# Transposing the first two batches of q and k head pair by head pair, in 64 by 64 blocks

## The chip, the core and the metric

The kernel runs on one core of a Trainium2 chip. The time is device time in microseconds (us) of one execution. Before the change the median of seven executions is 274.74 us (273.61 to 276.77). One further execution was recorded with the hardware profiler; it took 275.78 us, and its span, from the first to the last instruction, is 274.0 us. The clock granted to TensorE was 0.998 of full speed.

Engines are named as in the profile: PE (TensorE) does the matmuls, with PEld for its weight loads; DVE (VectorE), ACT (ScalarE) and POOL (GpSimd) do the rest of the arithmetic; SP (SyncE) issues nearly all of the transfers.

## What is computed

A causal attention over blocks of 64 positions is followed by a channel mix with two weight matrices and a gate. All inputs and the output are float32. The batch is 8, there are 8 heads, the sequence has 576 positions and a head has 64 columns.

```python
scores = (1 / sqrt(64)) * q @ k.T          # masked to block_i >= block_j
attn   = softmax(scores)
x      = (attn @ v)                        # heads side by side: 8 x 576 x 512
x_prev = x shifted by one position, zero first
xk = mu_k * x + (1 - mu_k) * x_prev
xr = mu_r * x + (1 - mu_r) * x_prev
kk = relu(xk @ w_k)                        # 512 -> 1024
out = sigmoid(xr @ w_r) * ((kk * kk) @ w_v)
```

## The kernel before

**Stages.** Scores are computed as keys by queries, so q and k are needed with the head's 64 columns on the partitions: the tile `t_qkt` holds, for each of four head pairs, 128 partitions, of which the upper 64 belong to one head and the lower 64 to another, for q and for k. The score matmuls (L774) contract over 64 partitions and alternate between the two heads of a pair, that is between the two halves of the partitions, writing two different PSUM banks. The exponential (L796, ACT) makes `t_e`, POOL sets masked pieces of it to zero (L805), and L839 multiplies it with v (`VO`; a column of ones gives the row sums). DVE normalises into `t_x` (L858, L859), TensorE transposes `t_x` (L913), and copies bring it to `t_xt`, which is cut into nine chunks of 512 positions. For each chunk `t_d` is the difference to the previous position (L952), `t_xk` and `t_xr` are two mixes of it (L964, DVE), and the three matrix products follow: L1000 with WK (then relu on ACT, L1010, and the square on DVE, L1016), L1029 with WR (tanh on ACT, L1039) and L1059 with WV, from which L1069 makes the output tile.

**Where q and k come from.** In batches 2 to 7 ("short rows") a transfer turns the rows: SP loads pieces, an engine casts them to bf16 (`NB`), and a transposing DMA writes `t_qkt`. In batches 0 and 1 (`LONGS = 2`, "long rows") TensorE does it. `add_long` loads with one transfer of 288 KB two neighbouring heads of q or k: partition `64*y + p` holds nine consecutive rows (576 numbers) of head y of the two. Two such transfers (x = 0 and 1) are cast into one tile `t_nl` of 128 x 9 x 128, x choosing the left or the right 64 of each 128 columns, so each cast writes pieces of 64 numbers. `add_long_qkt` then takes for each y the 64 partitions of that half and transposes nine blocks of 64 x 128 against a 64 x 64 identity (L704). Each result has 128 rows: 64 of the head of the first transfer, 64 of the head of the second. A pair in `t_qkt` therefore consists of heads from two transfers, and the function `heads` holds this other order of heads for these batches. An evacuation of 128 x 576 (L519 or L525) puts the nine blocks back into the order of positions.

**Order.** The kernel is a list of tasks, each with an engine, a planned duration, a rank, the tasks that it depends on and the ring buffers that it takes. `Plan.order` walks through planned time and gives each engine the free task of lowest rank; the result is a fixed order of instructions for each engine, and at run time every engine works its list strictly in order, waiting for data where it must. All ranks stand in the table `RANK`: `'loads'` is the order of SP's transfers for the first two batches and the weights (an entry such as `g0q` is two transfers, `v0` one of v, `wk3` a block of 256 KB of WK), the other entries move steps against each other, and `'eng'` chooses the engine for each cast, evacuation, copy and difference. L1000 of a chunk needs all four `t_xk` and four blocks of WK (for its first half, `wk0` to `wk3`), L1029 all four blocks of WR.

**Filler.** `fill` (L1098) is a pair of matmuls on the identity whose result nobody reads. 150 such tasks have the worst rank of all, so the plan puts them wherever TensorE has nothing else, until they are used up. They are 300 matmuls in TensorE's fixed list.

**Rings that matter here.** `ld` has ten buffers for all the float32 loads of q, k and weights, `vl` five for v; a transfer waits in SP's queue until its buffer is free, and the ones behind it wait too.

Of the kernel before, what the change touches and what calls it, by code (L numbers as in the profile page):

```python
# [9 lines left out]
FP = mybir.dt.float32  # L10
# [10 lines left out]
LONGS = 2  # L21
# [4 lines left out]
 'loads': ['g0q', 'v0', 'g0k', 'g1q', 'g1k', 'b1g1k', 'v4', 'wv3', 'wr3',  # L26
           'b1g0q', 'wk3', 'v2', 'v1', 'v3', 'b1g0k', 'wk2', 'wk4', 'wv5',
           'mu', 'b1v1', 'wk6', 'b1g1q', 'wr2', 'wv2', 'wk5', 'wv7',
           'b1v0', 'wv1', 'wr0', 'b1v2', 'b1v4', 'wk0', 'wk1', 'wv0',
           'wr1', 'b1v3', 'wk7', 'wv4', 'wv6'],  # L30
 'cast k': -51.0,
 'cast r': -434.5,
 'cast v': 313.0,
 'qkt0': [737.5, -314.0],
 'score0': [-705.0, -565.5, -372.0, -1059.0, -634.5, -690.5, -602.5,
            -488.0, -388.5, -812.5, -442.0, -834.5, -913.5],
 'av0': [-638.0, -695.5, -377.5, -465.0, -791.5, -541.5, -210.0, -635.5],
 'xt0': [-552.0, -461.5, -587.0, -627.5, -574.5],
 'mix0': [-254.0, 23.5, 351.5, 381.5],
 'pk0': [-136.5, 67.0, -206.0, -382.5, -79.5, -35.5, 48.0, -58.0],  # L40
 'pr0': [179.5, 182.0, -314.0, -81.5],
 'pv0': [15.0, -394.0, 22.5, 38.0],
 'qk': [38.0, 39.5, 41.5, 42.0],
 'v': 46.0,
 'qkt': [539.5, -136.5],
 'turn': 40.5,
 'av': -286.0,
 'xt': 6.0,
 'mix': 492.0,
 'xr': 423.5,  # L50
 'moe': 68.5,
 'eng': {'v32': 'DVE',
         'wk7': 'DVE',
         'qk201': 'POOL',
         'long0010': 'POOL',
         'v71': 'ACT',
         'd61': 'DVE',
# [3 lines left out]
         'd02': 'POOL',  # L61
         'd41': 'POOL',
         'v64': 'ACT',
         'qk511': 'POOL',
         'v72': 'POOL',
         'long0000': 'DVE',
         'd33': 'POOL',
         'qk611': 'POOL',
         'qk300': 'POOL',
         'd51': 'POOL',  # L70
         'v23': 'POOL',
         'long0110': 'DVE',
         'qk501': 'POOL',
         'd10': 'POOL',
         'ev0010': 'ACT',
         'v03': 'DVE',
         'd01': 'DVE',
         'long1110': 'POOL',
         'qk700': 'POOL',
         'v20': 'POOL',  # L80
         'v01': 'DVE',
         'qk601': 'POOL',
         'qk321': 'ACT',
         'v14': 'POOL',
         'qk620': 'ACT',
         'v51': 'DVE',
         'd20': 'POOL',
         'v41': 'POOL',
         'qk331': 'DVE',
         'qk430': 'POOL',  # L90
         'd32': 'POOL',
         'qk520': 'POOL',
         'long0001': 'ACT',
         'd53': 'DVE',
         'd81': 'POOL',
         'v73': 'POOL',
         'v40': 'POOL',
         'd31': 'DVE',
         'qk221': 'ACT',
         'd43': 'POOL',  # L100
# [3 lines left out]
         'qk730': 'ACT',  # L104
         'v21': 'POOL',
         'v54': 'POOL',
         'qk720': 'POOL',
         'wk6': 'DVE',
         'qk320': 'POOL',
         'd72': 'POOL',  # L110
         'v62': 'ACT',
         'd62': 'POOL',
         'qk500': 'POOL',
         'qk401': 'DVE',
         'v31': 'ACT',
         'd52': 'POOL',
         'long1111': 'POOL',
         'v63': 'POOL',
         'wk0': 'ACT',
         'qk411': 'POOL',  # L120
         'qk510': 'ACT',
         'long0011': 'ACT',
# [5 lines left out]
         'd82': 'DVE',  # L128
         'ev0000': 'ACT',
         'qk630': 'POOL',  # L130
         'v53': 'ACT',
         'v60': 'ACT',
         'v10': 'ACT',
# [3 lines left out]
         'qk421': 'POOL',  # L137
         'd11': 'POOL',
         'long1000': 'ACT',
         'qk310': 'POOL',  # L140
         'qk710': 'DVE',
         'long0111': 'ACT',
         'ev0101': 'ACT',
         'qk311': 'DVE',
         'wk2': 'DVE',
         'd71': 'POOL',
         'v52': 'POOL',
         'qk530': 'DVE',
         'qk220': 'DVE',
         'v04': 'POOL',  # L150
         'd73': 'POOL',
         'qk610': 'DVE',
         'd80': 'POOL',
         'long1100': 'ACT',
         'd60': 'POOL',
         'qk631': 'ACT',
         'qk600': 'DVE',
         'd83': 'POOL',
         'qk400': 'POOL',
         'v74': 'DVE',  # L160
         'v44': 'POOL',
         'v42': 'ACT',
         'long0100': 'DVE',
         'qk531': 'ACT',
         'long0101': 'DVE',
# [3 lines left out]
         'qk330': 'ACT',  # L169
         'd63': 'POOL',  # L170
         'qk231': 'POOL',
         'qk230': 'ACT',
         'v30': 'ACT',
         'd30': 'POOL',
         'qk711': 'POOL',
         'ev0001': 'ACT',
         'd50': 'POOL',
         'qk521': 'DVE',
         'long1101': 'POOL',
         'wk3': 'DVE',  # L180
         'qk431': 'POOL',
         'd00': 'POOL',
         'qk621': 'DVE',
         'qk731': 'POOL',
         'd03': 'POOL',
         'wk5': 'ACT',
         'qk410': 'DVE',
         'v02': 'POOL',
         'ev0011': 'ACT',
         'v34': 'ACT',  # L190
         'qk200': 'POOL',
         'long1001': 'POOL',
         'ev1011': 'ACT',
         'v22': 'POOL',
         'wk4': 'POOL',
         'wv4': 'ACT',
         'v11': 'POOL',
         'wr1': 'POOL',
         'v13': 'DVE',
         'long1010': 'ACT',  # L200
         'long1011': 'POOL',
         'v33': 'POOL',
         'wk1': 'ACT',
         'wv1': 'ACT',
         'd12': 'POOL',
         'ev1000': 'ACT',
         'wv2': 'ACT',
         'd13': 'DVE',
         'ev0111': 'ACT',
         'ev1010': 'ACT',  # L210
         'v12': 'POOL',
         'ev1101': 'DVE',
         'ev1111': 'ACT',
         'wv3': 'DVE',
         'd21': 'POOL',
         'ev0100': 'DVE',
         'ev1110': 'DVE',
         'wr0': 'DVE',
         'ev1001': 'DVE',
         'ev0110': 'DVE',  # L220
         'v24': 'POOL',
         'tail73': 'POOL',
         "xt('px', 3, 2)3": 'ACT',
         'tail72': 'DVE',
         "xt('px', 1, 4)2": 'DVE',
         "xt('px', 7, 0)7": 'ACT',
         "xt('px', 3, 3)4": 'DVE',
# [4 lines left out]
         'wv0': 'ACT',  # L232
         "xt('px', 7, 4)8": 'DVE',
         "xt('px', 4, 2)5": 'ACT',
         "xt('px', 4, 4)5": 'ACT',
         'tail33': 'DVE',
         "xt('px', 6, 2)7": 'DVE',
         "xt('px', 2, 0)3": 'ACT',
         "xt('px', 5, 2)6": 'ACT',
         'wv6': 'ACT',  # L240
         "xt('px', 2, 4)3": 'DVE',
         "xt('px', 4, 3)5": 'ACT',
         'tail21': 'POOL',
         'tail32': 'POOL',
         "xt('px', 7, 3)7": 'ACT',
         "xt('px', 5, 1)6": 'ACT',
         "xt('px', 2, 2)3": 'DVE',
         "xt('px', 7, 2)8": 'ACT',
         "xt('px', 6, 1)6": 'DVE',
         "xt('px', 1, 3)2": 'DVE',  # L250
         "xt('px', 4, 0)4": 'ACT',
         "xt('px', 5, 4)6": 'DVE',
         "xt('px', 2, 3)2": 'ACT',
         "xt('px', 3, 1)4": 'ACT',
         'tail62': 'DVE',
         "xt('px', 1, 3)1": 'ACT',
         "xt('px', 7, 0)8": 'ACT',
         "xt('px', 6, 2)6": 'ACT',
         'tail31': 'POOL',
         'tail22': 'ACT',  # L260
         "xt('px', 1, 1)2": 'DVE',
         "xt('px', 2, 0)2": 'DVE',
         'wv5': 'ACT',
         "xt('px', 5, 3)5": 'ACT',
         'tail43': 'DVE',
         "xt('px', 6, 0)7": 'ACT',
         "xt('px', 6, 0)6": 'ACT',
         "xt('px', 6, 4)7": 'ACT',
         'tail52': 'ACT',
         "xt('px', 5, 0)5": 'ACT',  # L270
# [4 lines left out]
         'tail42': 'POOL',  # L275
         "xt('px', 5, 1)5": 'ACT',
         "xt('px', 7, 2)7": 'ACT',
         "xt('px', 6, 3)6": 'ACT',
         'tail23': 'POOL',
         "xt('px', 6, 1)7": 'ACT',  # L280
         'tail60': 'POOL',
         "xt('px', 2, 3)3": 'DVE',
         "xt('px', 3, 4)4": 'ACT',
         "xt('px', 0, 3)0": 'DVE',
         "xt('px', 1, 1)1": 'DVE',
         'tail63': 'POOL',
         "xt('px', 4, 3)4": 'ACT',
         'tail70': 'POOL',
         "xt('px', 0, 4)1": 'DVE',
         "xt('px', 1, 2)2": 'ACT',  # L290
         "xt('px', 5, 0)6": 'DVE',
         "xt('px', 2, 1)3": 'ACT',
         'tail61': 'POOL',
         'tail71': 'POOL',
         'tail50': 'ACT',
# [3 lines left out]
         'tail30': 'ACT',  # L299
         "xt('px', 3, 2)4": 'DVE',  # L300
         "xt('px', 0, 2)0": 'DVE',
         "xt('px', 1, 0)1": 'ACT',
         "xt('px', 5, 3)6": 'ACT',
         'wv7': 'ACT',
         'tail53': 'POOL',
         "xt('px', 4, 1)5": 'ACT',
         'tail20': 'DVE',
         "xt('px', 3, 0)3": 'DVE',
         "xt('px', 4, 0)5": 'DVE',
         'tail40': 'DVE',  # L310
         'wr3': 'DVE',
         "xt('px', 0, 0)0": 'ACT',
         "xt('px', 2, 1)2": 'ACT',
         'tail51': 'DVE',
         "xt('px', 6, 3)7": 'ACT',
         "xt('px', 2, 2)2": 'ACT',
         "xt('px', 4, 2)4": 'DVE',
         'ev1100': 'ACT',
         "xt('px', 0, 1)0": 'ACT'},
# [94 lines left out]
def kernel(  # L414
# [28 lines left out]
    RINGS = {"ld": 10, "vl": 5, "nl": 4, "nb": 4, "tl": 2, "qkt": 2, "e": 3,  # L443
# [51 lines left out]
    def load(dst_key, make, jobs, rank, dur, deps=(), takes=(), uses=()):  # L495
        def fn():
            if make is not None:
                tiles[dst_key] = make()

            eng = nc.scalar if dst_key[:4] == ("ld", 0, 0, 1) else nc.sync  # L500
            for dst, src in jobs(tiles[dst_key]):
                eng.dma_start(dst, src)  # L502
        return plan.add("SP", dur, rank, fn, deps, takes, uses)
# [92 lines left out]
    def heads(b):  # L596


        return [4 * g + 2 * x + y if b < LONGS else 4 * g + 2 * y + x
                for g in range(2) for y in range(2) for x in range(2)]  # L600


    LONG = {(0, 0): ("DVE", "ACT"), (0, 1): ("POOL", "ACT"),
            (1, 0): ("DVE", "POOL"), (1, 1): ("POOL", "DVE")}
    CAST = {"POOL": 0.68, "DVE": 0.75, "ACT": 0.68}

    def add_long(b, g, ranks):


        for n, src in enumerate((q, k)):  # L610
            nb = plan.buf("nl")
            tiles["nbbuf", b, g, n] = nb
            cast["qk", b, g, n] = []
            for x in range(2):
                ld = plan.buf("ld")
                key = ("ld", b, g, n, x)
                t = load(key, lambda: new("ld", [P, S], FP),
                         lambda d, src=src, x=x: [
                             (d, src[b, 4 * g + 2 * x:4 * g + 2 * x + 2]
                              .rearrange("y (p j) d -> (y p) (j d)", j=JT))],  # L620
                         ranks[n], 0.85, takes=[ld])
                eng = LONG[g, n][x] if b == 0 else ("POOL", "DVE")[x]

                def fn(eng, n=n, key=key, x=x):
                    if x == 0:
                        tiles["nb", b, g, n] = new("nl", [P, JT, P], BF)
                    convert(eng, tiles["nb", b, g, n][:, :, x * D:x * D + D],
# [575 lines left out]
```

## Time and profile before

| | before |
|---|---|
| median of seven executions | 274.74 us |
| the profiled execution, its own time | 275.78 us |
| its span | 274.0 us |
| ACT, exponentials L796, 96 of 1028 ns | 95.7 us |
| PE, L1000, L1059, L1029 together | 172.1 us |
| DVE, strided casts to `t_nl`, 4 of 753 ns | 3.0 us |
| DVE, evacuations to `t_qkt`, 5 of 755 ns | 3.7 us |
| hardware DMA queue q1, share of 16 engines over the span | 82.3% |

Busy time is the time in which an engine executed something; a matmul's end is modelled, so matmuls that follow each other overlap by their tail of some 0.19 us. In the lines of a timeline or a chain the first number is the start, the second the length, both in us; `x18` counts instructions merged into one line; a bracket tells how long the engine had been idle before and what ended it. In the lines of groups the numbers after the bar are the busy time in us and the mean length of one in ns, then the idle time before them.

### The profile page before, as it was taken

The numbers are of one execution on the slowest core, as the hardware profiler recorded it, in microseconds if no ns is written. First come the engines' busy times: TensorE is split into PE (matmuls) and PEld (weight loads), VectorE is DVE, ScalarE is ACT, GpSimd is POOL, SyncE is SP. The second block draws the span as 40 slices with busy tenths as digits, with TensorE's granted clock in tenths as the row PEclk, the third lists the DMA queues.
The fourth block names the chain that finished last, engine by engine and source line by source line (L and its number), as shares of the span: only waits on it lengthen the run. The fifth ranks groups of instructions, "written<-read, shape, count | busy, mean of one in ns | idle before, by whom it ended". The sixth has DMA issues, their size and how long they took to land.

```text
span 274.0 us, 7012 instructions
## 1 busy us (share of the span) xinstructions
PE 263.4 (96%) x2676; PEld 152.4 (56%) x2676; DVE 210.3 (77%) x397; ACT 198.6 (72%) x311; POOL 113.2 (41%) x223
## 2 busy tenths in 40 slices
PE   8999988989999999999999999999999998999995
PEld 8877874546455555454555455555554655444443
DVE  3345897897987969976879699879975879996642
ACT  2599889985897978977898779778976782360630
POOL 3272572545666434654455426427454052410000
PEclk9999999999999999999999999999999999999999
DMA  7999999899999998899999989998997002202113
GB/s 227 329 293 242 297 285 216 178 204 254 244 191 209 197 249 198 182 216 238 216 211 217 242 203 206 212 236 199 209 206 216 2 0 76 79 0 94 61 42 115
DMA packets 137618, 51.33 MB, mean 187 GB/s; under 512 B 128240, under 2 KB 128496, under 8 KB 137584
## 3 DMA queue, kind: packets, MB, share of 16 engines
q1 hardware_dynamic: 137296, 50.29, 82.3%
q10 hardware_dynamic: 288, 0.59, 0.7%
q8 instruction: 21, 0.34, 0.5%
q14 instruction: 13, 0.11, 0.1%
HBM read 33.56 MB, written 9.44 MB: 157 GB/s over the span
## 4 chain that ended last, share of the span: by engine, by line
PE 79%; DVE 7%; DMA 6%; ACT 4%; issue 2%; SPq 1%; POOL 1%; POOLq 0%; DVEq 0%
PE t_mm L1000 21%; PE t_mm L1059 19%; PE t_mm L1029 10%; PE t_m L839 9%; PE t_s L774 7%; PE t_mm L1098 5%; PE t_m L913 5%; DMA out_dram<-t_o 3%; DMA t_ld<-in_moe_w_k_dram 2%; ACT t_e L796 2%; DVE t_xk L964 2%; DVE t_o L1069 1%; PE t_mm L839 1%; SPq L502 1%; ACT t_qkt L519 1%
## 5 line engine op out<-in xcount | busy, mean ns | idle before, releaser
L796 ACT ACTIVATE t_e<-t_s 128x1024 f16<-128x1024 f32 x96 | 95.7, 1028 | 12.5 <-PE t_s L774 10.1
L1000 PE MATMUL t_mm<-t_xk,WK 128*128 128x512 f16 x288 | 69.3, 380 | 2.3 <-ACT WK L519 1.6
L1059 PE MATMUL t_mm<-WV,t_k 128*128 128x512 f16 (+1 forms) x296 | 66.6, 373 | 1.0 <-DVE t_o L1069 1.0
L1016 DVE TENSOR_TENSOR t_k<-t_kr 128x512 f16<-128x512 f32 x72 | 54.5, 766 | 12.6 <-ACT t_kr L1010 12.0
L1010 ACT ACTIVATE t_kr<-t_mm 128x512 f32<-128x512 f32 x72 | 42.8, 599 | 16.4 <-PE t_mm L1000 15.8
L805 POOL MEMSET t_e<- 64x128 f16 (+1 forms) x96 | 23.3, 243 | 71.2 <-ACT t_e L796 68.8
L952 POOL TENSOR_TENSOR t_d<-t_xt 128x512 f32<-128x512 f32 x30 | 34.9, 1166 | 29.7 <-ACT t_xt L519 9.3
L1059 PEld LDWEIGHTS <-t_k 128*128 128x128 f16 x296 | 28.1, 98 | 32.6 <-issue 2.8
L1000 PEld LDWEIGHTS <-WK 128*128 128x128 f16 x288 | 25.9, 98 | 31.8 <-issue 4.2
L1069 DVE SCALAR_TENSOR_TENSOR t_o<-t_t,t_mm 128x512 f32<-128x512 f32 (+1 forms) x37 | 24.8, 669 | 18.2 <-PE t_mm L1059 11.4
L839 PEld LDWEIGHTS <-t_e 128*128 128x128 f16 x896 | 32.4, 97 | 9.9 <-issue 1.8
L1039 ACT ACTIVATE t_t<-t_mm 128x512 f32<-128x512 f32 x36 | 21.6, 600 | 21.9 <-PE t_mm L1029 20.9
L1029 PE MATMUL t_mm<-WR,t_xr 128*128 128x512 f16 x144 | 36.2, 380 | 0.1
L964 DVE SCALAR_TENSOR_TENSOR t_xk<-t_d,MUK,t_xt 128x512 f16<-128x512 f32 x36 | 30.7, 856 | 3.9 <-POOL t_d L952 3.8
L774 PE MATMUL t_s<-t_qkt 64*128 64x64 bf16 (+4 forms) x384 | 32.3, 277 | 1.2 <-ACT t_e L796 1.1
L839 PE MATMUL t_m<-VO,t_e 128*128 128x65 f16 x784 | 30.7, 193 | 0.8 <-POOL t_e L805 0.8
L964 DVE SCALAR_TENSOR_TENSOR t_xr<-t_d,MUR,t_xt 128x512 f16<-128x512 f32 x36 | 30.7, 869 | 0.0
L859 DVE TENSOR_TENSOR t_x<-t_m,t_r 128x320 f32<-128x320 f32 x56 | 27.5, 491 | 1.9
L774 PEld LDWEIGHTS <-t_qkt 64*128 64x128 bf16 x384 | 12.6, 94 | 21.3 <-issue 16.2
L1098 PE MATMUL t_mm<-identb 128*128 128x128 bf16 x300 | 22.4, 235 | 1.9 <-POOL identb masks.py:199 1.4
L525 POOL CAST NB<-t_ld 128x512 bf16<-128x512 f32 x27 | 19.7, 734 | 9.6 <-DMA t_ld<-in_q_dram 5.9
L913 PE MATMUL t_m<-identf,t_x 128*128 128x128 f32 x160 | 22.9, 276 | 0.2
(56 smaller groups left out, 231.5 us busy)
## 6 DMA issues: line engine op xcount, KB each, us to landing
out_dram<-t_o SPq DMA_DIRECT2D x35, 256.0 KB, 3.0
t_vl<-in_v_dram SPq DMA_DIRECT2D x32, 256.0 KB, 4.5
t_ld<-in_q_dram SPq DMA_DIRECT2D x48, 128.0 KB, 3.9
t_ld<-in_k_dram SPq DMA_DIRECT2D x48, 128.0 KB, 3.6
t_ld<-in_q_dram SPq DMA_DIRECT2D x8, 288.0 KB, 5.6
t_ld<-in_moe_w_v_dram SPq DMA_DIRECT2D x8, 256.0 KB, 6.5
t_ld<-in_moe_w_k_dram SPq DMA_DIRECT2D x8, 256.0 KB, 6.2
t_ld<-in_k_dram SPq DMA_DIRECT2D x6, 288.0 KB, 5.8
```

The source lines that it names most:

```text
L774: nc.tensor.matmul(PS[:, h, col:col + n], qkt[rows, pr, 1, kc * P:kc * P + P], qkt[rows, pr, 0, q0:q0 + n], start=True, stop=True)
L796: nc.scalar.activation(tiles["e", b, pr][:, :, i, :], tiles["ps", b, it], AF.Exp, scale=ISQ)
L839: nc.tensor.matmul(PA[:, mt * D1:(mt + 1) * D1], stationary(b, h, kc, mt), VOs[b % 2][:, kc, head, 0:D1], start=(kc == 0), stop=(kc == mt))
L913: nc.tensor.matmul(px[:, i * P:(i + 1) * P], src, identf, is_transpose=True, start=(i == 0), stop=(i == 3))
L952: (nc.vector if eng == "DVE" else nc.gpsimd).tensor_tensor(tiles["d", c, cc], x[:, cc, 1:CH + 1], x[:, cc, 0:CH], ALU.subtract)
L964: nc.vector.scalar_tensor_tensor(tiles[name, c][:, cc], tiles["d", c, cc], (MUK1, MUR1)[n][:, cc:cc + 1], tiles["xt", c][:, cc, 1:CH + 1], ...
L1000: nc.tensor.matmul(ps, WK[:, cc, jc * P:(jc + 1) * P], tiles["xk", c][:, cc], start=(cc == 0), stop=(cc == CCn - 1))
L1010: nc.scalar.activation(tiles["kr", c, jc], tiles["pk", c, jc], AF.Relu)
L1016: nc.vector.tensor_tensor(tiles["k2", c][:, jc], KR, KR, ALU.mult)
L1029: nc.tensor.matmul(ps, tiles["xr", c][:, cc, jt * P:(jt + 1) * P], WR[:, cc], start=(cc == 0), stop=(cc == CCn - 1))
L1059: nc.tensor.matmul(ps[:, 0:w], tiles["k2", c][:, jc, jt * P:(jt + 1) * P], WV[:, jc, cols], start=(jc == 0), stop=(jc == JCn - 1))
L1098: nc.tensor.matmul(ps[:, 384:512], identb, identb, start=True, stop=True)
```

## The change

For the two batches of long rows the work goes by pairs of neighbouring heads.

- `add_long` handles one pair `pr`: one transfer for q and one for k, each cast contiguously into a tile `t_nl` of 128 x 576.
- `add_long_qkt` transposes nine blocks of 64 x 64 for each of the two heads. The head in the upper 64 partitions is written to the upper 64 partitions of the PSUM tile, the one in the lower 64 to the lower 64: both use one PSUM bank, and they alternate. A task is now 18 transposes for q or for k of a pair (planned 0.5 us), where it was nine (planned 0.45 us).
- The evacuation keeps its shape; the order of heads is the plain one, and `heads` goes.
- The ring `nl` has eight tiles of half the size instead of four. Only one transfer of batch 0 goes through ACT's queue, the first of k, instead of two.
- The whole table `RANK` is replaced: the order of loads, all ranks, and the choice of engines for all batches.

```diff
 RANK = {
- 'loads': ['g0q', 'v0', 'g0k', 'g1q', 'g1k', 'b1g1k', 'v4', 'wv3', 'wr3',
-           'b1g0q', 'wk3', 'v2', 'v1', 'v3', 'b1g0k', 'wk2', 'wk4', 'wv5',
-           'mu', 'b1v1', 'wk6', 'b1g1q', 'wr2', 'wv2', 'wk5', 'wv7',
-           'b1v0', 'wv1', 'wr0', 'b1v2', 'b1v4', 'wk0', 'wk1', 'wv0',
-           'wr1', 'b1v3', 'wk7', 'wv4', 'wv6'],
+ 'loads': ['p0q', 'p0k', 'v0', 'p3q', 'b1p0q', 'p3k', 'p1k', 'wk2', 'p2q',
+           'wv4', 'p1q', 'b1p3k', 'v1', 'p2k', 'b1p0k', 'v3', 'v4', 'v2',
+           'wk0', 'b1p3q', 'b1p2k', 'b1p2q', 'wv3', 'wr0', 'wv1', 'b1v0',
+           'b1v2', 'wk5', 'b1v4', 'b1p1q', 'wv6', 'wr3', 'mu', 'wr1',
+           'b1p1k', 'wk4', 'b1v1', 'wk1', 'wv2', 'wk3', 'wv0', 'wk7',
+           'wv5', 'b1v3', 'wk6', 'wr2', 'wv7'],
...
-    RINGS = {"ld": 10, "vl": 5, "nl": 4, "nb": 4, "tl": 2, "qkt": 2, "e": 3,
+    RINGS = {"ld": 10, "vl": 5, "nl": 8, "nb": 4, "tl": 2, "qkt": 2, "e": 3,
...
-            for x in range(2):
-                ld = plan.buf("ld")
-                key = ("ld", b, g, n, x)
-                t = load(key, lambda: new("ld", [P, S], FP),
-                         lambda d, src=src, x=x: [
-                             (d, src[b, 4 * g + 2 * x:4 * g + 2 * x + 2]
-                              .rearrange("y (p j) d -> (y p) (j d)", j=JT))],
...
-                    convert(eng, tiles["nb", b, g, n][:, :, x * D:x * D + D],
-                            tiles[key][:, :].rearrange("p (j d) -> p j d", d=D))
+            t = load(key, lambda: new("ld", [P, S], FP),
+                     lambda d, src=src: [
+                         (d, src[b, 2 * pr:2 * pr + 2].rearrange(
+                             "h (p j) d -> (h p) (j d)", j=JT))],
+                     ranks[n], 0.85, takes=[ld])
...
+                tiles["nb", b, pr, n] = new("nl", [P, S], BF)
+                convert(eng, tiles["nb", b, pr, n], tiles[key])
...
-                    for j in range(JT):
-                        nc.tensor.matmul(
-                            pst[:, j * D:(j + 1) * D],
-                            tiles["nb", b, g, n][y * D:(y + 1) * D, j],
-                            identb[y * D:(y + 1) * D, y * D:(y + 1) * D],
-                            is_transpose=True,
-                            start=(j == 0), stop=(j == JT - 1))
-                t = on("PE", 0.45, rank + y, fn, cast["qk", b, g, n],
+                for j in range(JT):
+                    for h in range(2):
+                        rows = slice(h * D, h * D + D)
+                        nc.tensor.matmul(
+                            pst[rows, j * D:(j + 1) * D],
+                            tiles["nb", b, pr, n][rows, j * D:(j + 1) * D],
+                            identb[rows, rows], is_transpose=True,
+                            start=(j == 0), stop=(j == JT - 1))
+            t = on("PE", 0.5, rank, fn, [cast["qk", b, pr, n]],
...
-        head = heads(b)[h]
-        blk = head // 2
+        head, blk = h, pr
```

## The prediction

> **What bounds the kernel now.** I read the page's busy times, then its 40 slices, then the chain of waits in order of time, then TensorE's timeline around the first large matmul, last the groups by shape. From the page:
>
> ```profile
> PE 263.4 (96%) x2676; PEld 152.4 (56%) x2676; DVE 210.3 (77%) x397; ACT 198.6 (72%) x311; POOL 113.2 (41%) x223
> ...
> PE   8999988989999999999999999999999998999995
> ...
> DMA  7999999899999998899999989998997002202113
> ...
> L1098 PE MATMUL t_mm<-identb 128*128 128x128 bf16 x300 | 22.4, 235 | 1.9 <-POOL identb masks.py:199 1.4
> ```
>
> TensorE is the bound, but 22.4 of its 263.4 us are 300 filler matmuls (L1098), which compute nothing. The 5 us windows put all of them before 40 us. So TensorE's 274.0 us are about 241 of work, 22.4 of filler and 10.6 idle. The idle lies thus: 4.7 us up to the first full weight matmuls at 42.6, 3.1 in the last stretch (238 to 274 us, 32.9 busy), and some 2.8 over the whole middle. The middle is full; the change has to earn its time before 42 us. There:
>
> ```profile
> 35.46 6.44 DMA t_ld<-in_moe_w_k_dram
> 41.95 0.50 issue
> ```
> ```profile
> 38.67 0.84 PE L1098 MATMUL t_mm<-identb 128*128 128x128 bf16 x12
> 39.73 0.87 PE L774 MATMUL t_s<-t_qkt 64*128 64x512 bf16 x6 [0.22 <-ACT t_e L796]
> 41.91 0.39 PE L1000 MATMUL t_mm<-t_xk,WK 128*128 128x512 f16 x1 [1.30 <-ACT WK L519]
> 42.60 1.68 PE L1000 MATMUL t_mm<-t_xk,WK 128*128 128x512 f16 x7 [0.30 <-ACT WK L519]
> ```
>
> The first group of L1000 waits for the fourth block of WK, whose transfer took 6.44 us while the DMA engines are nearly saturated (9 in almost every slice). So the start is paced by the bytes ahead of WK in SP's queue, with the filler close behind: at 39 us TensorE was still running it.
>
> **The change part by part.** The order of the built kernel tells what the diff can't: filler stays 300, score matmuls 384, AV matmuls 960; long transposes go from 144 to 288.
>
> *Transposes.* The rows:
>
> ```profile
> L704 PE MATMUL t_m<-identb,t_nl 64*128 64x64 bf16 x144 | 5.2, 191 | 0.0
> L704 PEld LDWEIGHTS <-t_nl 64*128 64x128 bf16 x144 | 4.4, 95 | 0.9
> ```
> ```profile
> 8.62 0.60 PE L704 MATMUL t_m<-identb,t_nl 64*128 64x64 bf16 x18
> ```
> ```profile
> 22.23 0.29 PE L774 MATMUL t_s<-t_qkt 64*128 64x64 bf16 x8 [0.38 <-ACT t_e L796]
> ```
>
> Eighteen transposes, all in one half of the rows, last 0.60 with the tail of 0.19, so they start 0.41/17 = 24 ns apart; the following filler starts 0.52 after the first. Eight matmuls with the same 64 moving columns, alternating between the two row halves (L774), last 0.29: (0.29-0.19)/7 = 14 ns apart. Pairs in opposite halves do overlap in this trace, but those pairs write two different PSUM banks (`PS[:, h, ...]`), and the new ones write one. Here the Trainium skill ("TensorEngine Tiling (Array Packing)", Gotcha 1: PSUM Pressure) speaks against the change: different row tiles cannot access one PSUM bank at the same time. By the row, a task of 18 takes 17 x 0.014 + 0.11 (the gap to the next kind) = 0.35; by the rule 0.52, as now. Before there were 7 groups of 18 and 2 of 9 (about 0.36 each): 4.4 us. After there are 16 tasks: 5.6 by the row (+1.2), 8.3 by the rule (+3.9). I take the rule, because the row has no pair in one bank. The same page says that column tiling disables Fast Weight Load; "TensorE: Matmul & The Clock Gate" (LDWEIGHTS) prices a plain load at columns/1.2 ns, 53 ns for 64. If those loads ran one after another, a task would be 18 x 0.053 + 0.11 = 1.06 and the sum 17 us (+12.6). No row here has a load into a quarter of the array; that is the outer end.
>
> *Casts.* Sixteen on each side. On DVE a strided one took 753 ns (four); a contiguous one is nearest DVE's WK cast, 428 ns for 512 columns, so 480 for 576. DVE has six now: 3.0 becomes 2.9. POOL goes from six to nine (692 ns each, +2.1), ACT from six to one (674, -3.4). Evacuations stay sixteen: ACT 11 to 8 at some 0.6, DVE 5 to 8 at 755 ns (+2.3). ACT, full from 21 to 28 us, is relieved. DVE up to the fourth t_xk of chunk 0 has 28.5 us by its listed instructions, against 24.5 before, of some 40: covered, unless it falls into the last 8 us, where DVE was full.
>
> *One transfer brings a pair of heads.* The first scores need two transfers of 288 KB, not four; the k one is alone on ACT's queue, and SP issues one more (about 0.45). But filler stands in front by its count: 68 matmuls, not 82. The 82 took 7.32; the last 14 of them at 59 ns are 0.8, so the first transposes start at 7.9 instead of 8.7, although their data should be there by 5.5. The first scores follow at about 10.5 (two tasks, 18 fillers, an evacuation), 12.43 before. Filler takes back most of the lead.
>
> *To the first AV.* From 7.9: 112 fillers at 59 ns 6.6, 11 transpose tasks 5.7 (3.9 by the row), 38 score matmuls in 8 blocks at 0.3 to 0.5, 3.0: 23.2 (21.4). ACT's own list (eight exponentials of 1.03, evacuations, EL, VO) from 10.7 ends at 21.5. First AV 23.5 (before 23.6); 21.7 by the row.
>
> *To the first WK matmul.* 120 AV 3.6, 120 fillers 7.0, five transpose tasks 2.6 (1.8), 44 score matmuls 3.3, five t_x groups 2.3: 18.8 (18.0). That gives 42.3 (39.7), plus waits; the same stretch held 2.4 us of them before; with TensorE later I take 1.5: 43.8. By the row the bytes decide: WK is complete after 10,240 KB in the queue (wk3) instead of 10,496 (wk1), at some 280 GB/s 0.9 us sooner: landing at 40.5, then a cast and one t_xk on DVE (0.43 + 0.86), 42.0. WR is complete 768 KB later (2.8 us, near 46), and its first use stands 4.4 us behind the first WK matmul: just covered.
>
> Ten more score matmuls (0.54 + 0.36) are done by then. Against 42.2 (41.91 and the 0.30): 43.8 - 0.9 - 42.2 = **+0.7**; by the row 42.0 - 0.9 - 42.2 = -1.1.
>
> *The middle and the tail.* All ranks and engine choices of batches 2 to 7 change too. Counting each form by its duration, DVE ends 0.5 us lighter, ACT 7 lighter, POOL 6 heavier; TensorE's work is the same, and the order of its last hundred matmuls too. A new order can win at most the 2.8 us of idle there; it can lose more, since each engine works its list in order and DVE, ACT and the output buffers each held TensorE up once or twice (0.81 at 56, 0.44 at 127, 0.69 at 225 us). I take +1.2, bounds -2.5 and +5.
>
> **The sum.** +0.7 + 1.2 = +1.9 us on the span of 274.0. The profiled execution took 275.78, 1.8 more than its span; the median of seven is 274.74. On the median: 276.6.
>
> **The rivals.**
> 1. *Pairs overlap and the bytes of WK pace the start* (the other side): -1.1 there; it decides as soon as a task of 18 stays under some 0.45 us, since TensorE's list then ends before WK lands. For it: the 14 ns row, WK's place in the queue, ACT's relief. Against: nothing here shows two tiles in one bank. With -1.5 in the middle as well, because batch 1 starts with ten scores more and ACT with three casts fewer: 272.1.
> 2. *The same, but the middle gives it back* (+1.2): 274.8, no change.
> 3. *Weight loads into a quarter are slow*: 17 us of transposes, 8.7 more than by the rule; all of it beyond 42.3 is uncovered, so the first WK matmul comes near 52 and the time is about 284. It decides as soon as a task takes over 0.8 us. Against: alternating halves load weights 13 ns apart in the L774 row.
>
> **Chances.** Forecast (slower, one bank serializes and the new order stalls a little) 0.42, its own range 275.4 to 279.5; rival 1 0.30; rival 2 0.20; rival 3 0.08. About 0.5% (1.4 us) is what a measurement tells from no change. So faster 0.30, same 0.20, slower 0.50. The range leaves out rival 3 and the far end of rival 1: 271.6 to 281.
>
> **What would show it.** A transpose group of 18 lasting 0.6 (serial), 0.43 (paired) or over 1 us (slow loads); first transposes at 7.9, first scores near 10.5, first AV near 23.5, first WK matmul at 43.8 and what it waits for: TensorE's own list (mine) or the DMA of WK (rival 1). Idle on TensorE from 45 to 238 us above 3 us would be the middle's loss. A first WK matmul before 41, or idle in the middle under 2 us, would make me wrong.

## The result, and the profile after

The changed kernel takes **279.59 us** (median of 12 executions, 278.75 to 282.0); the kernel before, run with it, takes 275.14 (median of 31). The ratio is **1.018**, with a 95% interval of 1.0154 to 1.0206: slower, by 4.45 us in the medians. (The ratio is one of means and leaves out the three longest executions of the kernel before; the medians alone give 1.016.) Its profiled execution took 281.45 us with a span of 279.7, which is 5.7 more than the span before.

The line numbers have moved: L988 is the product with WK (L1000 before), L1017 that with WR, L1047 that with WV, L1057 the output tile (L1069), L1063 its transfer (L1075), L998 relu and L1004 the square, L763 the scores, L694 the long transposes, L1086 the filler. The page:

```profile
PE 266.4 (95%) x2820; PEld 153.9 (55%) x2820; DVE 213.8 (76%) x397; ACT 193.5 (69%) x302; POOL 120.3 (43%) x232
...
PE   8999899999999999999999999959998999999995
...
PEclk9999999999999999999999999989999999999999
```

The row of slices shows the difference by itself: one slice of TensorE at 5 in the middle (the 27th, 182 to 189 us), where before none but the last was under 8, and in the same slice the only 8 in the row of the granted clock. The start, where the prediction looked for the change, reads as follows (TensorE's timeline):

```profile
7.32 0.47 PE L694 MATMUL t_m<-identb,t_nl 64*64 64x64 bf16 x18
...
9.34 0.61 PE L763 MATMUL t_s<-t_qkt 64*128 64x512 bf16 x6
...
40.71 1.74 PE L1086 MATMUL t_mm<-identb 128*128 128x128 bf16 x28
42.38 0.61 PE L763 MATMUL t_s<-t_qkt 64*128 64x512 bf16 x6
42.92 0.60 PE L988 MATMUL t_mm<-t_xk,WK 128*128 128x512 f16 x2
```

TensorE runs filler, then scores, then the first weight matmul with no bracket of idle time: its own list sets 42.92, not the bytes of WK. With the ten more score matmuls done by then (0.9), and against 42.2 before, the start ends level: 42.92 - 0.9 - 42.2 = -0.2.

So the loss lies behind 43 us. Busy time by stretches (length, then TensorE, its weight loads, DVE, ACT, POOL, the granted clock, the DMA share and GB/s), first before, then after:

```profile
43.00:238.00 195.00, 192.26 (x1861) 104.76 (x1860) 161.82 (x312) 153.23 (x244) 92.39 (x176) 1.00 0.93 190
```
```profile
43.00:238.00 195.00, 188.13 (x1829) 102.92 (x1830) 157.03 (x300) 150.21 (x241) 91.99 (x173) 0.99 0.89 187
```

Idle time of TensorE, worked out from these rows, from those of the two other stretches and from the spans (the last column is the kernel of experiment e8, below):

| idle TensorE, us | before | after | e8 |
|---|---|---|---|
| 0 to 43 | 4.7 | 3.0 | 2.2 |
| 43 to 238 | 2.7 | **6.9** | **0.2** |
| 238 to the end | 3.1 | 3.4 | 3.4 |
| busy, whole span | 263.4 | 266.4 | 262.9 |

**Followed back from TensorE.** What TensorE waited for from 42 us on (in all, times, longest):

```profile
PE t_mm L988 <- DVE t_o L1057: 3.7, 2, 3.3
PE t_mm L988 <- ACT t_kr L998: 2.7, 4, 0.7
```

And what DVE's L1057 itself waited for:

```profile
DVE t_o L1057 <- DMA out_dram<-t_o: 11.5, 4, 4.3
```

The kernel before has the same two waits, but shorter:

```profile
PE t_mm L1000 <- DVE t_o L1069: 0.7, 2, 0.4
DVE t_o L1069 <- DMA out_dram<-t_o: 4.5, 3, 1.9
```

The longest of these waits, in DVE's timeline, SP's list and the chain of waits of the changed kernel:

```profile
180.22 0.67 DVE L1057 SCALAR_TENSOR_TENSOR t_o<-t_t,t_mm 128x512 f32<-128x512 f32 x1
185.20 0.69 DVE L1057 SCALAR_TENSOR_TENSOR t_o<-t_t,t_mm 128x512 f32<-128x512 f32 x1 [4.31 <-DMA out_dram<-t_o]
185.81 0.68 DVE L1004 TENSOR_TENSOR t_k<-t_kr 128x512 f16<-128x512 f32 x1
```
```profile
179.34 0.56 SPq L1063 DMA_DIRECT2D out_dram<-t_o  x1
179.95 0.61 SPq L503 DMA_DIRECT2D t_tl<-in_q_dram  x1
180.60 0.67 SPq L503 DMA_DIRECT2D t_tl<-in_k_dram  x1
181.31 2.15 SPq L503 DMA_DIRECT2D t_ld<-in_q_dram  x2
183.50 1.84 SPq L503 DMA_DIRECT2D t_ld<-in_k_dram  x2
185.45 1.46 SPq L1063 DMA_DIRECT2D out_dram<-t_o  x3
```
```profile
179.34 5.73 DMA out_dram<-t_o
185.07 0.03 issue
...
185.20 0.70 DVE t_o L1057
185.90 0.04 issue
185.94 2.94 PE t_mm L988 x8
```

Read from the bottom up. TensorE starts L988 at 185.94 after 3.27 us of nothing. It needs one of the two PSUM tiles `mm`: that one still held the last product of L1047 (done near 181.2), and L1057 is what reads it. L1057 stood at the head of DVE's list, which works in order, and waited for a place in the ring of output tiles, which has three. (Which of the two `mm` tiles a group takes is fixed when the kernel is built, so the other one, emptied by relu at 183.3, was no help.) The three output tiles were full: one had been on its way since 179.34 and landed 5.73 us later, with six loads issued behind it; the two others stood in SP's list behind those loads and were issued only at 185.45. Everything behind waits too: ACT idles 3.43 us before its next relu at 187.21, and DVE's square L1004 comes at 185.81.

SP's list has the same pattern, one output, six loads, three outputs together, at 94, 122 and 150 us, and four outputs in a row at 212. At 98.3 and 154.1 DVE waits 2.0 us for `out_dram`, at 216.4 it waits 3.1. There TensorE loses less, 0.69 each (the row of ACT t_kr; at 98.6, 126.7, 154.9 and 215.6): its next group takes the tile that relu empties, because the other is still held. At 126.8 the profile puts DVE's wait down to ACT instead. Before, at 177 to 194 us, the outputs were issued one at a time between the loads, the fourth at 193.20. From SP's list of the kernel before:

```profile
177.59 0.61 SPq L1075 DMA_DIRECT2D out_dram<-t_o  x1
...
181.40 1.06 SPq L502 DMA_DIRECT2D t_ld<-in_k_dram  x2
182.55 0.53 SPq L1075 DMA_DIRECT2D out_dram<-t_o  x1
...
184.34 1.05 SPq L502 DMA_DIRECT2D t_ld<-in_k_dram  x2
...
188.49 0.63 SPq L1075 DMA_DIRECT2D out_dram<-t_o  x1
```

After the gap TensorE runs slower. Its eight L988 take 2.94 us here and 1.89 at 98.6. The windows of 7 us (TensorE's busy time, granted clock, DMA share, GB/s):

```profile
175.00:182.00 7.00, 7.00 (x50) 1.00 1.04 224
182.00:189.00 7.00, 3.73 (x16) 0.83 0.92 226
189.00:196.00 7.00, 7.00 (x92) 0.93 0.35 77
```

By estimate from these two rows 7 x 0.17 + 7 x 0.07 = 1.7 us are lost to the lower clock (1.05 of it shows in those eight matmuls). In windows of 1 us the granted clock is 1.00 up to 186 us, then 0.81, 0.50 from 187 to 190, and 0.98 after that. Not in every execution: five of the twelve have a mean clock of 0.992 to 0.994, and a median of 281.2; the seven others have 0.998 to 1.000 and 279.2. The median of all, +4.45, is thus nearly the idle time alone: -0.2 at the start, +4.1 in the middle (6.87 - 2.74), +0.3 at the end.

### The profile page after: what moved, and what is told of

The parts are those of the page before. It is cut to its first block, busy times and chain, and to the rows that moved or that the text cites. A ratio compares the mean times of both kernels' runs of the same rounds, so it can differ in the third digit from the quotient of the medians.

```text
span 279.7 us, 7305 instructions
## 1 busy us (share of the span) xinstructions
PE 266.4 (95%) x2820; PEld 153.9 (55%) x2820; DVE 213.8 (76%) x397; ACT 193.5 (69%) x302; POOL 120.3 (43%) x232
## 4 chain that ended last, share of the span: by engine, by line
PE 79%; DMA 6%; DVE 5%; SPq 3%; issue 3%; ACT 2%; POOL 1%; DVEq 0%; POOLq 0%; ACTq 0%
PE t_mm L988 20%; PE t_mm L1047 18%; PE t_mm L1017 9%; PE t_s L763 8%; PE t_m L827 8%; PE t_mm L1086 7%; PE t_m L901 5%; DMA out_dram<-t_o 5%; SPq L503 3%; PE t_m L694 2%; PE t_mm L827 1%; DMA t_ld<-in_q_dram 1%; DVE t_o L1057 1%; DVE t_nl L526 1%; ACT t_e L785 1%
## 5 line engine op out<-in xcount | busy, mean ns | idle before, releaser
L785 ACT ACTIVATE t_e<-t_s 128x1024 f16<-128x1024 f32 x96 | 97.1, 1032 | 18.9 <-PE t_s L763 18.4
L988 PE MATMUL t_mm<-t_xk,WK 128*128 128x512 f16 x288 | 70.2, 384 | 6.5 <-DVE t_o L1057 3.7
L1047 PE MATMUL t_mm<-WV,t_k 128*128 128x512 f16 (+1 forms) x296 | 66.6, 373 | 0.3 <-DVE t_o L1057 0.3
L1004 DVE TENSOR_TENSOR t_k<-t_kr 128x512 f16<-128x512 f32 x72 | 54.4, 767 | 14.6 <-ACT t_kr L998 14.1
L998 ACT ACTIVATE t_kr<-t_mm 128x512 f32<-128x512 f32 x72 | 43.0, 598 | 22.6 <-PE t_mm L988 21.8
L794 POOL MEMSET t_e<- 64x128 f16 (+1 forms) x96 | 23.5, 245 | 75.6 <-ACT t_e L785 67.9
L940 POOL TENSOR_TENSOR t_d<-t_xt 128x512 f32<-128x512 f32 x31 | 37.6, 1214 | 26.3 <-ACT t_xt L520 10.7
L988 PEld LDWEIGHTS <-WK 128*128 128x128 f16 x288 | 26.3, 98 | 37.5 <-issue 11.9
L1047 PEld LDWEIGHTS <-t_k 128*128 128x128 f16 x296 | 27.9, 98 | 32.6 <-issue 2.8
L1057 DVE SCALAR_TENSOR_TENSOR t_o<-t_t,t_mm 128x512 f32<-128x512 f32 (+1 forms) x37 | 24.7, 668 | 24.5 <-DMA out_dram<-t_o 11.5
L1017 PE MATMUL t_mm<-WR,t_xr 128*128 128x512 f16 x144 | 36.5, 379 | 0.0
L763 PE MATMUL t_s<-t_qkt 64*128 64x64 bf16 (+4 forms) x384 | 32.5, 280 | 0.0
L952 DVE SCALAR_TENSOR_TENSOR t_xr<-t_d,MUR,t_xt 128x512 f16<-128x512 f32 x36 | 32.4, 915 | 0.0
L952 DVE SCALAR_TENSOR_TENSOR t_xk<-t_d,MUK,t_xt 128x512 f16<-128x512 f32 x36 | 29.0, 812 | 2.2 <-POOL t_d L940 2.1
L520 ACT COPY t_xt<-t_m 128x256 f32<-128x256 f32 (+7 forms) x46 | 16.8, 396 | 12.1 <-PE t_m L901 9.7
L1086 PE MATMUL t_mm<-identb 128*128 128x128 bf16 x300 | 22.9, 232 | 1.8 <-POOL identb masks.py:199 1.4
```

The source lines that it names most:

```text
L763: nc.tensor.matmul(PS[:, h, col:col + n], qkt[rows, pr, 1, kc * P:kc * P + P], qkt[rows, pr, 0, q0:q0 + n], start=True, stop=True)
L785: nc.scalar.activation(tiles["e", b, pr][:, :, i, :], tiles["ps", b, it], AF.Exp, scale=ISQ)
L940: (nc.vector if eng == "DVE" else nc.gpsimd).tensor_tensor(tiles["d", c, cc], x[:, cc, 1:CH + 1], x[:, cc, 0:CH], ALU.subtract)
L952: nc.vector.scalar_tensor_tensor(tiles[name, c][:, cc], tiles["d", c, cc], (MUK1, MUR1)[n][:, cc:cc + 1], tiles["xt", c][:, cc, 1:CH + 1], ...
L988: nc.tensor.matmul(ps, WK[:, cc, jc * P:(jc + 1) * P], tiles["xk", c][:, cc], start=(cc == 0), stop=(cc == CCn - 1))
L998: nc.scalar.activation(tiles["kr", c, jc], tiles["pk", c, jc], AF.Relu)
```

## The experiments

**e1: the changed kernel once more**, unedited, to see which waits belong to the kernel and which to one execution.

> The changed kernel once more, for a second recorded execution. Theory 'middle' (the loss lies behind 43 us, where the new order of batches 2 to 7 makes TensorE wait): again about 279.5, first WK matmul near 42.9 and some 4 us more idle or half-clock time than before between 43 and 238 us, though the single 3.3 us stall of the first recording may stand elsewhere or be split. Theory 'start' (transposes, filler and DVE up to the first WK matmul): a first WK matmul clearly later than 43 and a middle like that of the kernel before.

280.4 us, ratio 1.0166 [1.0092, 1.0239]. The first weight matmul is at 43.02, the stall at 183 to 186 us is there again with 2.4 us, and the four waits of 0.69 on relu too. They belong to the order. The slow casts are there too, but differ (below).

**e2, e3, e4: exchanging the middle by the table.** e2 gives the changed kernel the ranks and engines that batches 2 to 7 had before; e3 gives the kernel before those of the changed one; e4 gives the changed kernel the old engines alone.

```diff
# e2
- 'turn': -206.0,  'av': -357.0,  'xt': -49.5,  'mix': 471.0, ...
+ 'turn': 40.5,    'av': -286.0,  'xt': 6.0,    'mix': 492.0, ...
- 'eng': {'v32': 'POOL', 'qk201': 'DVE', 'd61': 'POOL', ...
+ 'eng': {'v32': 'DVE', 'qk201': 'POOL', 'd61': 'DVE', ...
# e3: the same entries of the kernel before, the other way round
# e4: only 'eng'
```

> The changed kernel with the table entries that order and place batches 2 to 7 (qk, v, turn, av, xt, mix, xr, moe, and the engines of 184 tasks of these batches) as in the kernel before; the instructions up to the first WK matmul stay as they are. Theory 'middle': 274.5 to 276.5. Theory 'start': 279 or more. If the mixed table orders badly in itself: above 279.

> The opposite: the kernel before, with its own start, and the changed kernel's entries for batches 2 to 7. Theory 'middle': 277.5 to 280. Theory 'start': 274 to 275.5.

> The changed kernel with only the engine choices of batches 2 to 7 from the kernel before (casts, evacuations and differences), ranks as changed. If the choice of engines makes the middle's loss (tail casts on ACT, output tiles late on DVE): 275 to 277. If the ranks make it: 279.

280.07 (1.017 [1.0115, 1.0224]), 282.29 (1.0252 [1.0167, 1.0337]) and 282.54 (1.0263 [1.0195, 1.033]). e3 and e4 lie outside all of their ranges; e2 lies where 'start' or a table that orders badly would put it. The table is not a list of instructions: with half of it exchanged, the plan is made anew and comes out with other waits. In e2 TensorE waits for relu (1.7 us) and for POOL's masks (1.3), in e3 for exponentials (2.3) and a mix on POOL (1.6), and in e4 for such mixes above all:

```profile
PE t_mm L984 <- POOL t_xk L963: 4.3, 4, 1.6
```

They don't tell structure and order apart. What follows is only that the old engine choices alone don't mend the new kernel.

**e5, e6, e7: the order written out.** Instead of planning, these kernels issue their tasks by a fixed list. In e5 it is the order and the engines of the kernel before, with the new blocks of 64 x 64 put where the old transposes stood; e6 takes the new order for the start and the old one for the rest, e7 the reverse.

```diff
-    for t in plan.order():
-        t["fn"]()
+    for i in ORDER:
+        plan.tasks[i]["fn"]()
```

> The changed structure (a pair per transfer, contiguous casts, 64 by 64 transposes in one bank) with the task order and the engines of the kernel before, written out as a list instead of planned: every task stands where its counterpart stood, only each transpose task has 18 matmuls instead of 9. Theory 'order' (the structure costs nearly nothing, the re-made order of the whole kernel costs the 4.5 us): 274 to 276.5, the +2 us of TensorE time for 144 more transposes being partly hidden in the start. Theory 'structure': 278 to 280.

> The changed kernel up to its first WK matmul exactly as it is, after that every task in the order and on the engine of the kernel before. Theory 'middle' (the loss is in the order behind 43 us): 274 to 276. Theory 'start': 278 to 280.

> The opposite: the kernel before up to its first WK matmul, after that the order and engines of the changed kernel. Theory 'middle': 278 to 281, with the wait for an output tile near 183 us. Theory 'start': 274.5 to 276.

e5: 277.21 us, ratio 1.0067 [1.0034, 1.01], between the two ranges. So the new structure by itself costs some 2 us, at the start: the first weight matmul stands at 43.96, against 41.91 before, since TensorE has 288 transposes in place of 144 and nothing else has moved. TensorE's transposes are busy 6.4 us (5.2 before); the other 0.8 of the delay I didn't follow. The rest of the loss, 277.2 to 279.6, must be the order, with three output tiles.

e6 and e7 (282.56, 1.0277 [1.0206, 1.0348]; 283.82, 1.0286 [1.0209, 1.0364]) were to say whether start or rest of the new order is to blame, and their times don't: the halves don't fit. In e6 the seam itself stalls for 5.4 us,

```profile
PE t_mm L1101 <- ACT t_kr L1082: 5.4, 1, 5.4
```

and TensorE is busy only 20.25 us of the 27 from 43 to 70. In e7 TensorE waits 1.5 us for `t_x`, 0.2 in the changed kernel. A cut through an order that was planned as one adds stalls of the size that is sought. The traces do say where the output tiles run out: DVE's waits for `out_dram` are 14.8 us in e7 and 4.6 in e6 (11.5 in the changed kernel, 4.5 in the kernel before), so they go with the new order behind 43 us.

**e8: a fourth output tile**, the instructions on every engine in the same order. To make room, `nl` has seven tiles instead of eight.

```diff
-            tc.tile_pool(name="p_" + n, bufs=bufs, **kw))
+            tc.tile_pool(name="p_" + n, bufs={"o": 4, "nl": 7}.get(n, bufs), **kw))
```

> The changed kernel with four output tiles instead of three (and seven small t_nl tiles instead of eight, for the space); the order of instructions is the same. If TensorE's stall of 2.4 to 3.3 us near 184 us and the slower clock after it come from an output tile that waits for a transfer which SP issued late: the stall goes, 275 to 277. If that stall is only one of many symptoms: above 278.

**272.06 us** (four executions, 270.56 to 273.33), ratio to before 0.9891 [0.9831, 0.9952]: 7.5 us less than the changed kernel, more than was expected, and about 1% faster than the kernel before. No wait of L1057 for `out_dram` is left in the trace. What remains of output tiles among TensorE's waits is

```profile
PE t_mm L1047 <- DVE t_o L1057: 0.3, 1, 0.3
```

and the stretches where the changed kernel stalled are full, at a full clock:

```profile
43.00:238.00 195.00, 194.76 (x1872) 106.77 (x1871) 167.02 (x313) 153.22 (x247) 96.04 (x175) 1.00 0.85 188
```
```profile
182.00:189.00 7.00, 7.00 (x81) 1.00 1.01 258
```

SP's list is as before the edit, one output at 174.67 and three together at 180.84: the same transfers in the same order hurt nobody when DVE has one tile more.

**e9: seven `nl` tiles alone** (`{"nl": 7}`), the part of e8's edit that should do nothing.

> The changed kernel with seven t_nl tiles instead of eight and still three output tiles: the other half of the edit before. If the fourth output tile did it: 279 to 281, stall near 184 us as before. If the place of tiles in memory or the t_nl ring did it: 272 to 274.

279.44 us, 1.0161 [1.0104, 1.0218], the stalls as in the changed kernel (TensorE stands for 2.73 us before 185.82):

```profile
DVE t_o L1057 <- DMA out_dram<-t_o: 12.2, 5, 3.8
```

The output tile made the difference in e8.

**e10: four output tiles in the kernel before** (`{"o": 4, "nl": 3}`); **e11: e5 with four output tiles** (`{"o": 4, "nl": 7}`). Is the tile worth something in any order?

> The kernel before with four output tiles (and three of its double-size t_nl tiles instead of four, for the space). Its three waits of output tiles for a transfer are 4.5 us on DVE, of which 1.7 reach TensorE. Theory 'only the new order runs out of output tiles': 273 to 275. Theory 'the fourth tile is worth as much in either kernel': 267 to 270, and the changed kernel would be the slower one at equal rings.

> The changed structure in the task order of the kernel before, with four output tiles and seven t_nl tiles. With three it was 277.2 and TensorE waited 1.9 us for output tiles. Theory 'the structure costs 2 us in the start and the order decides the rest': 275 to 276.5, so 3 us behind the new order with four tiles. If four tiles are worth 7 us in any order: 269 to 271.

274.95 us, 1.0005 [0.9982, 1.0027]; and 276.77, 1.0064 [1.0037, 1.0091]. Both are as with three tiles (e11 lies just above its range). The kernel before does wait for output tiles on DVE (the 4.5 us), but only 1.7 us of waiting for L1069 reach TensorE, and 1.0 of that is still there in e10, so next to nothing is to be had. With e5, e8 and e9 this makes a table of medians:

| | three output tiles | four |
|---|---|---|
| old blocks, old order | 275.14 | 274.95 |
| new blocks, old order (e5, e11) | 277.21 | 276.77 |
| new blocks, new order (after, e8) | 279.59 | 272.06 |

The blocks cost about 2 us in either column. The new order is worth -4.7 us with four tiles and +2.4 with three.

**e12: heads not alternating**, on top of e8: each task does its nine transposes of one head, then the nine of the other, so that those which follow each other stand in the same quadrant.

```diff
-                for j in range(JT):
-                    for h in range(2):
+                for h in range(2):
+                    for j in range(JT):
```

> The changed kernel with four output tiles, but in each transpose task first the nine blocks of one head, then the nine of the other, so that neighbours share a quadrant instead of standing in opposite ones. If opposite quadrants overlap although they write one bank: a task goes from 0.40 us to 0.50 or more, 1.6 us and more over 16 tasks, and the time to 273 to 274. If one bank serializes them anyway: tasks stay at 0.40 and the time at 272.

274.73 us, 0.9982 [0.9961, 1.0003]: 2.7 us more than e8, somewhat above the range for overlap. A task of 18, in e8 and then in e12:

```profile
7.42 0.47 PE L694 MATMUL t_m<-identb,t_nl 64*64 64x64 bf16 x18
7.82 1.07 PE L1086 MATMUL t_mm<-identb 128*128 128x128 bf16 x16
```
```profile
7.34 0.65 PE L694 MATMUL t_m<-identb,t_nl 64*64 64x64 bf16 x18
7.92 1.07 PE L1086 MATMUL t_mm<-identb 128*128 128x128 bf16 x16
```

Alternating, they start (0.47 - 0.195)/17 = 16 ns apart and the filler follows 0.40 after the first; in succession (0.65 - 0.195)/17 = 27 ns and 0.58. Sixteen tasks at 0.18 make 2.9 us, about the difference of the times; the first weight matmul moves from 41.29 to 44.67. So the shared PSUM bank doesn't hold opposite quadrants to the pace of one quadrant: they overlap. Whether the matmuls or their weight loads set the 27 ns within a quadrant, these rows don't separate.

**Not tried, or open.** e8's start is also 1.6 us earlier than that of the changed kernel (41.29 against 42.92; 42.90 in e9). The first output is far behind that point, so this part of e8's gain isn't explained by the stalls above. In the old order the traces with four tiles start earlier too (40.80 in e10 against 41.91 before, 42.35 in e11 against 43.96 in e5), where the medians differ by 0.2 and 0.4 only, and the recorded executions of e8 and e11 are the shortest of their kernels, e8's 1.5 us under its median. So it may belong to these executions; the cause stays open. The new order was not run with the old blocks, so its worth is known with the new ones alone. And e8 has four executions only: that it beats the kernel before rests on an interval that ends at 0.9952.

## Why the prediction was right or wrong

The direction was right, and the time is inside the range of 271.6 to 281, though just past the forecast's own (275.4 to 279.5); the size was not right: +1.9 us were forecast and +4.45 came (the median of before, run again, is 275.14 instead of 274.74).

- **The step that failed: "I take +1.2" for the middle.** It measured +4.1 us of idle TensorE, and 1.7 more of lowered clock in the profiled execution: the first is inside the bound of +5 that stood beside it, the two together are not. The prediction named the output buffers as one of three things that "each held TensorE up once or twice", and then priced all three by the before trace, where they were small. What it did not do was follow SP's new list, which was there with the order of the built kernel: the outputs are no longer spread between the loads, but one stands ahead of six loads and three behind them, four times. The order could be read without a run. What it costs follows with the run's times: even with the median landing before, 3.0 us, the tile of 179.34 comes free at 182.3, some 1.5 us after DVE has got to the next L1057 (180.9), and at 94, 122 and 150 us it is 1.0 to 1.1. The landing of 5.7 us, with six loads issued behind it, only the run shows. The plan can't see it, because it takes an output tile as free shortly after its transfer is issued:

```python
...
on("SP", 0.7 / parts, rank, ..., [t], uses=[o])
...
u["free"] = max(u["free"] or 0.0, t["end"] + 0.1)      # in Plan.order
```

  0.7 + 0.1 = 0.8 us, where the trace shows a median of 3.5 us from issue to landing after the change, and up to 5.7. So the order holds a stall that the plan's own arithmetic doesn't contain.
- **Bank or row: the rule was the wrong choice.** The prediction weighed 0.52 a task (by the Trainium skill, "TensorEngine Tiling (Array Packing)", Gotcha 1: no two row tiles in one bank at a time) against 0.35 (by the row of alternating score matmuls), and took the rule. Measured: 0.40, with e12 beside it at 0.58. Sixteen tasks are 6.4 us instead of 4.4, +2.0, where +3.9 was booked by the rule and +1.2 by the row. As a limit on the pace the rule doesn't show for two opposite quadrants of a bank. The prediction's own argument against the row, that no pair there wrote one bank, was sound; no row could decide it.
- **Start: near, by errors that cancel.** First transposes 7.32 (7.9 forecast), first scores 9.34 (10.5), first weighted sums 22.32 (23.5), first WK matmul 42.92 (43.8); balance -0.2 instead of +0.7. With the first transposes 0.6 earlier and each task at 0.40 (16 x 0.12 = 1.9 less), the forecast's sum would have given 41.3, where the trace of e8 has it; the changed kernel is 1.6 later, 0.7 of that ahead of the first weighted sums and 0.9 behind. Two brackets of idle time in the second stretch (0.41 and 0.93, both for DVE) are known, but 1.5 were allowed for waits. That TensorE's own list and not the bytes would set the point was right (the last cast of WK ahead of it ended at 41.80), and WR was covered as said.
- **Casts: 480 ns were right for a cast alone, and half of them were not alone.** The group on DVE is

```profile
L526 DVE CAST t_nl<-t_ld 128x576 bf16<-128x576 f32 x6 | 5.5, 917 | 1.4 <-DMA t_ld<-in_k_dram 1.4
```

  a mean of 917 ns, 5.5 us for the six where 2.9 were booked: three took 0.45, the others 0.65, 1.09 and 2.41. The one at 31.97 us took 2.41; a copy stood behind it on DVE (34.30), and TensorE's transposes at 34.76 had waited 0.93 us for that copy.
- **Rival 1** ("a task of 18 stays under some 0.45 us", so the bytes decide) had its condition met, 0.40, and still did not come about: TensorE's list ended after WK had landed. Its time of 272.1 is what e8 gives, but by another way: with 0.2 us of idle time in the middle. **Rival 2** had the same +1.2 for the middle, which was too little. **Rival 3** (slow weight loads) is out: 16 ns between starts, and 27 within a quadrant (e12), not 53.
- **What would show it** named the right window: "Idle on TensorE from 45 to 238 us above 3 us would be the middle's loss".

## What to carry to other kernels

An order that was planned is only as good as the plan's idea of when a buffer comes free: before it is believed, walk the transfer queue's list, and for each ring ask how many tiles the consumer needs before the first write has landed, with the landing time that the trace shows and what is queued in front. One wait on an engine that works in order goes through all that stands behind it, so trace a stall of the busiest engine back engine by engine until a DMA or a ring ends it. When a new order comes out slower, give the starved ring one tile more with the order unchanged before rejecting it: here that turned +4.45 us into -3.

## What the runs showed of the hardware

- **Opposite quadrants of one PSUM bank** are written by matmuls that overlap: 64 x 64 blocks that alternate between rows and partitions 0 to 63 and 64 to 127 start 16 ns apart, the same blocks within one quadrant 27 ns apart (e8, e12).
- **A contiguous DVE cast** of 128 x 576 from fp32 to bf16 takes 0.45 us alone (460 ns is the mean of four in e5), but from 0.65 to 2.41 in the changed kernel wherever POOL was at work beside it. DVE, then POOL in the same time:

```profile
24.25 0.45 DVE L526 CAST t_nl<-t_ld 128x576 bf16<-128x576 f32 x1
...
30.43 1.20 DVE L528 TENSOR_SCALAR WV<-t_ld 128x512 f16<-128x512 f32 x1
...
31.97 2.41 DVE L526 CAST t_nl<-t_ld 128x576 bf16<-128x576 f32 x1
```
```profile
31.83 0.68 POOL L526 CAST VO<-t_vl 64x512 f16<-64x512 f32 x1
32.48 1.03 POOL L940 TENSOR_TENSOR t_d<-t_xt 128x512 f32<-128x512 f32 x1
33.46 0.60 POOL L526 CAST WR<-t_ld 128x512 f16<-128x512 f32 x1
```

  POOL has three operations under the 2.41 us, and the cast ends 0.32 us after the last of them (34.38 and 34.06). It does so in every trace of this order: the same cast took 1.52 us in e1, 1.86 in e8, 2.41 in e9 and 3.02 in e12, and ended 0.31 to 0.32 us after an operation of POOL each time, as if it had waited for POOL to pause. The Trainium skill ("GPSIMD Engine Reference", Specifications) has the two engines share their way to SBUF, with contention for some of DVE's instructions; these rows fit that, but no run here took POOL's work away, so the cause is not shown.
- **An idle gap and the clock after it.** 2.4 to 3.3 us of idle TensorE, once, were followed by a granted clock of 0.77 to 0.83 over the 7 us that hold the gap and 0.93 to 0.99 over the next 7 (after and e1); the gaps of 0.69 at 98.6, 126.7 and 154.9 us left it at full. Of the 22 executions of the kernels with that gap (after, e1, e9) 12 have a mean clock of 0.992 to 0.994; of the 26 of e8 and e12, which have no gap of 0.6 us behind 43 us in their traces, none has. But the kernel before has it too, in 13 of the 55 that ran beside e9 to e12, and those are 1.7 us longer (medians of 276.74 and 275.01), with no gap above 0.81 us behind 43 us in its trace. So the gap is not the only way to the lower clock, and that it is the cause is not shown.
